# Tokens of a pair of rows split over even and odd partitions, loads reordered, q transposed by the DMA crossbar: a fused linear attention and MLP-mixer kernel on one Trainium2 core

## The chip, the cores and the metric

The kernel runs on one core of a Trainium2 chip. The metric is the device time of one execution in microseconds (us), lower is better. Beside every timed kernel the kernel before is run on the same chip. Its executions fall into two groups, about 321 to 323 us and about 325.5 to 329 us. Runs more than 1.5% above the fastest of the same kernel are called slow here, and only fast runs are compared. The span of a profiled execution is about 1.8 us shorter than its device time.

Engines: PE is TensorE, DVE is VectorE, ACT is ScalarE, POOL is GpSimd, SP is the sync engine, which issues most DMAs. In the traces SP, ACT and POOL each issue to a DMA queue of their own (SPq, ACTq, POOLq). PSUM is the memory that the matmuls write here. The "crossbar" stands for `dma_start_transpose`: a DMA that transposes what it moves. A DMA "lands" when all its data has arrived. The "granted clock" is the share of full speed that TensorE's clock was given.

## The reference

For 8 batches of 576 tokens, with 8 heads of 64 and 1536 channels in the MLP:

```python
r_q, r_k = relu(q), relu(k)                      # [8, 8, 576, 64]
q_p = concat(r_q * cos(pos), r_q * sin(pos))     # 128 features per head
k_p = concat(r_k * cos(pos), r_k * sin(pos))
kv  = sum over tokens of k_p (outer) v ;  z = sum over tokens of k_p
x   = (q_p @ kv) / (q_p . z + 1e-6)              # -> [8, 576, 512], heads side by side
h   = relu(x^T @ w_tok1) @ w_tok2                # mix over tokens
u   = x + h^T
out = u + relu(u @ w_ch1) @ w_ch2                # mix over channels
```

All matmuls are in bf16, inputs and output in float32.

## The kernel before: the parts that matter

576 tokens are 4.5 times 128 partitions. The kernel gives 5 tokens to each of 64 partitions and 4 to each of the other 64. In even batches the 5-token half is partitions 0 to 63, in odd batches 64 to 127, so that two batches' fifth tokens ("tails") together fill 128 partitions for the channel MLP. A tail tile alone has 64 rows.

```python
def halves(c):                        # c = batch % 2
    lo = c * HP                       # HP = 64
    return slice(lo, lo + HP), slice(HP - lo, P - lo)

def load(b, t):                       # two DMAs, two queues, one half each
    A, Bh = halves(b % 2)
    ...
    qB = nc.scalar if b == 0 else nc.gpsimd
    return [nc.sync.dma_start(out=x[A], in_=...),            # 64 partitions x 5 tokens
            qB.dma_start(out=x[Bh, :, :J * D], in_=...)]     # 64 partitions x 4 tokens

def q_turn(self, g):                  # q features -> transposed, for the matmul with kv
    ...
    tr = psA.tile([P, 2 * H, P], BF16, ...)
    for i in range(2 * H):
        nc.tensor.transpose(tr[:, i, :], src[:, i * P:(i + 1) * P], ident)
    nc.scalar.copy(dst, tr)           # 16 PE transposes, one ACT copy out of PSUM
    # g == 2: the tail, 64 rows, 8 transposes

def num(self, j):                     # r is all rows for j < 4, the half A for the tail
    for h in range(H):
        nc.tensor.matmul(nm[r, ...], lw, self.kv[:, h, :D + 1], ...)
```

A period is one batch's channel MLP (48 c_ps matmuls with w_ch1, 48 o_ps matmuls with w_ch2). The attention and the token mixing of the next batch (in the code the steps kv, num, mix1 and mix2, with the tiles kv_ps, nm, b, u_ps and ut_ps) and the q transposes (tr) of the one after are hooked in between, so that PE is always busy. Batch 0 has to be prepared first, and in the first two periods batches 1 and 2 are still being loaded. From batch 2 on, u is transposed by the DMA crossbar; q never is.

## Time and profile before

Device time: 324.75 us median of 4 runs; 321.77 and 322.38 are the fast ones, 327.11 and 327.18 the slow ones. The profiled execution was a fast one. A "third period" below is the third MLP block, counted from its first c_ps matmul. (In the tables of the kernel before and the changed kernel the bounds from the fourth period on come from the chain of waits and lie some 0.16 us later; lengths of whole periods do not change.)

| Stretch of the profiled execution | us | what holds it |
|---|---|---|
| start to the first c_ps | 34.6 | loads of batch 0, then a chain over all engines |
| first period | 46.8 | loads of batch 1, PE clock |
| second period | 40.0 | loads of batches 2 and 3 |
| third period | 32.5 | PE |
| fourth to sixth, each | 30.7 | PE |
| seventh (no q transposes left) | 28.5 | PE |
| the last two blocks and the stores | 46.3 | PE |

The page's head and its slices. A digit is a tenth of busy time in one of 40 slices of the span, PEclk the clock granted to PE in tenths, GB/s what the DMA engines moved:

```profile
span 320.8 us, 5010 instructions
PE 287.4 (90%) x2032; PEld 145.8 (45%) x2056; DVE 165.9 (52%) x326; ACT 141.1 (44%) x184; POOL 62.7 (20%) x97
...
PEclk9789978799999997999999999999999999999999
DMA  7899999910999899914797299622063105302214
GB/s 155 286 140 220 240 259 279 229 25 4 213 281 278 168 264 256 211 42 109 178 255 145 66 231 236 126 65 67 0 67 88 47 0 120 95 0 65 67 36 95
```

PE's 90% is an average over stages with different limits and says little. Two other things are seen: the clock digits 7 and 8 in the first quarter, and the ninth and tenth slice (64 to 80 us), where DMA moves 25 and 4 GB/s although the second period will wait for loads. The stretches from the view by windows (length; busy time and instructions of PE, PEld, DVE, ACT, POOL; granted clock; DMA share; GB/s), for the first, second, fourth and seventh period, confirm it:

```profile
34.57:81.38 46.81, 35.78 (x251) 18.15 (x253) 23.83 (x48) 22.61 (x30) 7.90 (x13) 0.89 0.74 171
81.38:121.40 40.02, 33.51 (x273) 17.61 (x276) 24.57 (x46) 20.96 (x25) 14.94 (x22) 1.00 1.03 242
153.86:184.58 30.72, 30.56 (x235) 15.77 (x236) 17.71 (x36) 17.76 (x23) 6.92 (x10) 1.00 0.73 168
246.03:274.53 28.50, 28.39 (x195) 13.76 (x196) 13.77 (x26) 6.40 (x10) 2.70 (x3) 1.00 0.25 61
```

The chain of waits (start, length, what) has long DMA links before 121 us, and afterwards PE without a break:

```profile
42.17 21.86 DMA w_112<-w_111
...
84.11 20.70 DMA vt<-in_v_dram
...
114.13 7.23 DMA uT<-ub
```

The DMA queue of SP (start, length, what) shows why nothing moved at 64 to 80 us. The load of k for batch 3 stands behind a crossbar transpose that needs the end of the first period:

```profile
78.61 1.28 SPq L314 DMA_TRANSPOSE uT_tail<-utb  x1
80.00 0.65 SPq L76 DMA_DIRECT2D kt<-in_k_dram  x1
```

The rates of the first 20 us, half a microsecond for each number. Batch 0's halves come on two queues, and the rate lies near 210 for five microseconds before it rises:

```profile
GB/s 0 0 0 0 96 78 217 356 229 205 241 233 218 207 203 201 258 332 342 379 390 389 370 376 384 395 386 344 236 13 0 0 0 0 92 179 142 167 58 141
```

### The profile page before, as it was taken

The page shows a single profiled execution, that of the slowest core. Times are in us where ns is not written, and L with a number is a line of the kernel's source. Part 1 is how long each engine was busy: PE and PEld are TensorE (multiplying, and loading weights), DVE is VectorE, ACT ScalarE, POOL GpSimd, SP SyncE. Part 2 cuts the span into 40 slices and gives each one's busy share as a digit, 9 for nine tenths or more (in the row PEclk, how much of TensorE's full clock was granted, in tenths as well). Part 3 has the DMA queues.
Part 4 walks back from the last instruction along what each step waited for, and adds up shares of the span by engine and source line. Part 5 has one row for each costly group of instructions (what it writes and reads, how often), then busy time and mean ns, then how long its engine had stood idle before and what let it go on. Part 6 is the DMA issues. An engine that isn't in the chain of part 4 may idle for free.

```text
span 320.8 us, 5010 instructions
## 1 busy us (share of the span) xinstructions
PE 287.4 (90%) x2032; PEld 145.8 (45%) x2056; DVE 165.9 (52%) x326; ACT 141.1 (44%) x184; POOL 62.7 (20%) x97
## 2 busy tenths in 40 slices
PE   7488874898887978999999999999999999999993
PEld 3263432543553435445544564455455544444441
DVE  0846582237754960666356655765564753332421
ACT  2280439109649142395349445935673420220300
POOL 1077003005510651030602050700020012000000
PEclk9789978799999997999999999999999999999999
DMA  7899999910999899914797299622063105302214
GB/s 155 286 140 220 240 259 279 229 25 4 213 281 278 168 264 256 211 42 109 178 255 145 66 231 236 126 65 67 0 67 88 47 0 120 95 0 65 67 36 95
DMA packets 39127, 45.78 MB, mean 143 GB/s; under 512 B 16448, under 2 KB 33600, under 8 KB 39104
## 3 DMA queue, kind: packets, MB, share of 16 engines
q1 hardware_dynamic: 30880, 29.14, 39.3%
q0 software_dynamic: 6640, 14.75, 21.4%
q10 hardware_dynamic: 1584, 1.57, 1.7%
q8 instruction: 16, 0.26, 0.4%
q14 instruction: 7, 0.06, 0.1%
HBM read 35.78 MB, written 9.44 MB: 141 GB/s over the span
## 4 chain that ended last, share of the span: by engine, by line
PE 70%; DMA 18%; DVE 5%; issue 2%; POOL 2%; ACT 1%; SPq 1%; POOLq 0%; DVEq 0%
PE c_ps L342 25%; PE o_ps L365 23%; DMA w_112<-w_111 7%; DMA vt<-in_v_dram 6%; PE u_ps L295 3%; PE tr L220 3%; PE kv_ps L237 3%; PE nm L253 3%; DMA kt<-in_k_dram 3%; DMA uT<-ub 2%; DVE kp L182 2%; PE o_ps L354 2%; PE ut_ps L308 1%; PE wm L117 1%; POOL vbf_109 L192 1%
## 5 line engine op out<-in xcount | busy, mean ns | idle before, releaser
L342 PE MATMUL c_ps<-uT,wc_117 128*128 128x512 bf16 x384 | 95.9, 387 | 8.4 <-ACT uT L326 2.4
L342 PEld LDWEIGHTS <-wc_117 128*128 128x128 bf16 x432 | 39.4, 99 | 53.6 <-issue 11.9
L207 ACT ACTIVATE qp<-qt,bias_93,cos_t 128x512 bf16<-128x512 f32 (+1 forms) x40 | 31.6, 805 | 17.1 <-DMA qt<-in_q_dram 12.1
L301 POOL CAST ub<-u 128x1024 bf16<-128x1024 f32 x14 | 14.8, 1054 | 122.6 <-DVE u L300 122.6
L368 DVE TENSOR_TENSOR u<-o_ps,u 128x512 f32<-128x512 f32 x28 | 19.3, 691 | 37.5 <-PE o_ps L365 33.6
L221 ACT COPY qpT<-tr 128x2048 bf16<-128x2048 bf16 x16 | 29.9, 1867 | 18.7 <-PE tr L220 18.7
L257 DVE TENSOR_SCALAR den<-nm 128x8 f32<-128x8 f32 (+1 forms) x40 | 6.6, 165 | 42.3 <-PE nm L253 41.8
L261 DVE TENSOR_TENSOR x<-nm,den 128x512 bf16<-128x512 f32 (+1 forms) x40 | 27.6, 691 | 1.4
L182 DVE TENSOR_SCALAR kp<-kt,cos_t 128x512 bf16<-128x512 f32 (+1 forms) x40 | 21.2, 531 | 10.7 <-DMA kt<-in_k_dram 10.7
L207 ACT ACTIVATE qp<-qt,bias_93,sin_t 128x512 bf16<-128x512 f32 (+1 forms) x30 | 24.0, 800 | 0.0
L220 PE MATMUL tr<-ident,qp 128*128 128x128 bf16 x256 | 17.9, 225 | 4.6 <-DVE qp L204 4.4
L182 DVE TENSOR_SCALAR kp<-kt,sin_t 128x512 bf16<-128x512 f32 (+1 forms) x40 | 21.7, 543 | 0.0
L220 PEld LDWEIGHTS <-qp 128*128 128x128 bf16 x256 | 15.9, 101 | 9.2 <-ACT qp L207 5.0
L300 DVE TENSOR_TENSOR u<-u_ps,x 128x1024 f32<-128x1024 f32 x14 | 17.1, 1219 | 2.3 <-PE u_ps L295 2.3
L192 POOL CAST vbf_109<-vt 128x512 bf16<-128x512 f32 (+1 forms) x18 | 11.2, 655 | 31.0 <-DMA vt<-in_v_dram 16.3
L237 PEld LDWEIGHTS <-kp 128*128 128x128 bf16 (+1 forms) x320 | 13.9, 108 | 5.3 <-ACT qpT L221 1.8
L253 PEld LDWEIGHTS <-qpT 128*128 128x128 bf16 x256 | 12.1, 98 | 9.1 <-DVE x L261 2.4
L253 PE MATMUL nm<-kv,qpT 128*128 128x65 bf16 x256 | 13.4, 194 | 1.6 <-DVE x L261 1.6
L117 PE MATMUL wm<-zero 128*128 128x512 bf16 x39 | 12.0, 458 | 2.1 <-DVE zero L111 2.0
L346 ACT ACTIVATE h_2979<-c_ps 128x512 bf16<-128x512 f32 x6 | 3.6, 597 | 21.0 <-PE c_ps L342 21.0
L354 PE MATMUL o_ps<-wc_121,h_429 128*128 128x512 bf16 x45 | 12.5, 396 | 0.2
L365 PE MATMUL o_ps<-wc_121,h_826 128*128 128x512 bf16 x46 | 11.6, 380 | 0.8 <-ACT h_826 L346 0.8
(123 smaller groups left out, 378.0 us busy)
## 6 DMA issues: line engine op xcount, KB each, us to landing
out_dram<-u SPq DMA_DIRECT2D x32, 256.0 KB, 3.3
kt<-in_k_dram SPq DMA_DIRECT2D x8, 640.0 KB, 11.2
qt<-in_q_dram SPq DMA_DIRECT2D x8, 640.0 KB, 14.4
vt<-in_v_dram SPq DMA_DIRECT2D x8, 640.0 KB, 14.5
kt<-in_k_dram POOLq DMA_DIRECT2D x7, 512.0 KB, 6.9
qt<-in_q_dram POOLq DMA_DIRECT2D x7, 512.0 KB, 8.4
vt<-in_v_dram POOLq DMA_DIRECT2D x7, 512.0 KB, 10.5
wc_117<-in_moe_w_ch_dram POOLq DMA_DIRECT2D x3, 512.0 KB, 9.3
```

The costliest lines, as they stand in the source:

```text
L182: nc.vector.tensor_scalar(self.kp[r, j, :, f, :], src, scalar1=tab[r, self.c, j:j + 1], scalar2=0.0, op0=ALU.mult, op1=ALU.max)
L207: nc.scalar.activation(self.qp[r, j, :, f, :], src, AF.Relu, bias=bias0[r], scale=tab[r, self.c, j:j + 1])
L220: nc.tensor.transpose(tr[:, i, :], src[:, i * P:(i + 1) * P], ident)
L221: nc.scalar.copy(dst, tr)
L237: nc.tensor.matmul(kv_ps[:, g, hh * (D + 1):(hh + 1) * (D + 1)], self.kp[r, j, h].rearrange("p f d -> p (f d)"), self.vb[r, j, h, :D + 1], ...
L253: nc.tensor.matmul(nm[r, h // HH, c0:c0 + D + 1], lw, self.kv[:, h, :D + 1], start=True, stop=True)
L261: nc.vector.tensor_mul(self.x[r, j, :].rearrange("p (g h d) -> p g h d", g=2, h=HH), nmv[r, :, :, :D], den_b[r])
L300: nc.vector.tensor_add(self.u[:, js, :], u_ps, self.x[:, js, :])
L342: nc.tensor.matmul(c_ps, wc1[:, ki, mi * P:(mi + 1) * P], uT[:, :, ki, :], start=(ki == 0), stop=(ki == NCC - 1))
L354: nc.tensor.matmul(o_ps[j], h1[:, ki, j * P:(j + 1) * P], wc2[:, ki, :], start=(ki == 0), stop=(ki == NCH - 1))
L365: nc.tensor.matmul(o_ps, h1[:, ki, j * P:(j + 1) * P], wc2[:, ki, :], start=(ki == 0), stop=(ki == NCH - 1))
L368: nc.vector.tensor_add(u[:, j, :], o_ps, u[:, j, :])
```

## The change

Its intent: spread each load over even or odd partitions instead of 64 neighbouring ones; get data into the first two periods sooner; and take the q transposes of batches 3 to 7 off PE and ACT.

Tokens are grouped in 64 runs of 9. A run's 5 and 4 tokens go to a pair of neighbouring partitions. A tail tile now lies on every second partition and is handled as 128 rows, of which 64 are zero.

```diff
-    Q_DMA = ()
+    Q_DMA = range(3, 8)
@@ load
-        return [
-            nc.sync.dma_start(out=x[A], in_=...),
-            qB.dma_start(out=x[Bh, :, :J * D], in_=...),
-        ]
+        for par in (1 - b % 2, b % 2):
+            n, f = count(b % 2, par), first(b % 2)[par]
+            dmas.append(nc.sync.dma_start(
+                out=x[par::2, :, :n * D],
+                in_=src[b].rearrange("h (m r) d -> m h (r d)", r=R)[:, :, f * D:(f + n) * D]))
@@ order of loads
-    after(first w_tok1 load, v0[0])
+    after(first w_tok1 load, q0[1])
 ...  k, q, v of batch 1
+    (copy of w_tok1 for odd batches)        # was behind k, q of batch 2
     w_ch2 in four parts                     # now after q of batch 1
     k, q of batch 2                         # now after part 3 of w_ch2
-    (copy of w_tok1 for odd batches)
@@ q_turn
-            if g < J // 2: ... crossbar or 16 transposes, else: the tail, 64 rows
+        src = self.qp[:, j:j + n] ...
+        if self.b in Q_DMA:
+            nc.sync.dma_start_transpose(out=dst, in_=src)
+            return
@@ kv_mm, num, mix1, mix2: every tail
-            r = self.rows(j)          # 64 rows for the tail
-                nc.tensor.matmul(nm[r, ...], lw, ...)
+                nc.tensor.matmul(nm[:, ...], lw, ...)
@@ start: batch 0
-    s.q_turn(0)                       # 16 transposes at once, later 16 and 8 more
+        s.q_turn(j, 1, psM)           # 8 at a time, between the num steps
@@ first period: v casts, kv and num one or two slots later, and
-        (the load of k, q of batch 3 stood behind the transpose of u_tail)
+        (it stands before it)
```

Cut: the cos and sin tables for the new token places, clearing of the unused tail columns, the same slicing of weights and stores, three v casts of batch 1 that go from POOL to DVE, and the slots of the other hooks.

More of the change, by code (lines that the diff above doesn't have):

```diff
@@ L34 @@
     P = 128
-    HP = P // 2
     J = S // P
     JA = J + 1
-    SA = HP * JA
+    R = J + JA
     NP = B // 2
@@ L44, with first, count @@
     VW = D + 2
-    Q_DMA = ()
+    Q_DMA = range(3, 8)
     U_PE = (0, 1)
-    def halves(c):
-        lo = c * HP
-        return slice(lo, lo + HP), slice(HP - lo, P - lo)
+    def first(c):
+        return (0, JA - c)
+    def count(c, par):
+        return JA if par == c else J
     const = ctx.enter_context(tc.tile_pool(name="const", bufs=1))
@@ L61, with clear, raw_of @@
     ctx.enter_context(tc.manual_schedule())
-    raw = {}
-    def load(b, t):
-        A, Bh = halves(b % 2)
-        if t == "v":
-            x = one.tile([P, H, JA * D], F32, name="vt", tag="vt")
-        else:
-            x = two.tile([P, H, JA * D], F32, name=t + "t", tag=t + "t")
-        src = {"q": q, "k": k, "v": v}[t]
-        raw[t, b] = x
-        qB = nc.scalar if b == 0 else nc.gpsimd
-        return [
-            nc.sync.dma_start(out=x[A], in_=src[b, :, :SA, :].rearrange("h (p j) d -> p h (j d)", j=JA)),
-            qB.dma_start(out=x[Bh, :, :J * D], in_=src[b, :, SA:, :].rearrange("h (p j) d -> p h (j d)", j=J)),
-        ]
+    raw = {(t, i): const.tile([P, H, JA * D], F32, name=f"{t}t{i}") for t, i in
+           (("k", 0), ("q", 0), ("v", 0), ("k", 1), ("q", 1))}
+    def clear(t, i):
+        (nc.gpsimd if t == "q" else nc.vector).memset(raw[t, i][:, :, J * D:], 0.0)
+    for t in "kqv":
+        clear(t, 0)
+    def raw_of(t, b):
+        return raw[t, 0 if t == "v" else b % 2]
+    def load(b, t):
+        x = raw_of(t, b)
+        src = {"q": q, "k": k, "v": v}[t]
+        dmas = []
+        for par in (1 - b % 2, b % 2):
[3 more added lines that the diff above has]
+                in_=src[b].rearrange("h (m r) d -> m h (r d)", r=R)[:, :, f * D:(f + n) * D]))
+        return dmas
     def after(dma, first):
@@ L86 @@
     load(0, "k")
-    load(0, "q")
-    v0 = load(0, "v")
-    pos_i = const.tile([P, 2, JA], mybir.dt.int32, name="pos_i")
-    for c in range(2):
-        A, Bh = halves(c)
-        nc.gpsimd.iota(pos_i[A, c, :], pattern=[[1, JA]], base=0, channel_multiplier=JA)
-        nc.gpsimd.iota(pos_i[Bh, c, :], pattern=[[1, JA]], base=SA, channel_multiplier=J)
+    q0 = load(0, "q")
+    load(0, "v")
+    pos_i = const.tile([P, JA], mybir.dt.int32, name="pos_i")
+    nc.gpsimd.iota(pos_i, pattern=[[2, JA]], base=0, channel_multiplier=R)
+    par_i = const.tile([P, 1], mybir.dt.int32, name="par_i")
+    nc.gpsimd.iota(par_i, pattern=[[0, 1]], base=0, channel_multiplier=1)
+    nc.vector.tensor_single_scalar(par_i, par_i, 1, op=ALU.bitwise_and)
+    par = const.tile([P, 1], F32, name="par")
+    nc.vector.tensor_copy(par, par_i)
+    keep = const.tile([P, 2], F32, name="keep")
+    nc.vector.tensor_scalar(keep[:, 0:1], par, scalar1=-1.0, scalar2=1.0, op0=ALU.mult, op1=ALU.add)
+    nc.vector.tensor_copy(keep[:, 1:2], par)
+    pos = const.tile([P, JA], F32, name="pos")
+    nc.vector.tensor_copy(pos, pos_i)
     theta = const.tile([P, 2, JA], F32, name="theta")
-    nc.vector.tensor_copy(theta, pos_i)
-    scale = (math.pi / 2.0) / S
+    nc.vector.tensor_scalar(theta[:, 0, :], pos, scalar1=par, scalar2=None, op0=ALU.add)
+    nc.vector.tensor_scalar(theta[:, 1, :], pos, scalar1=par, scalar2=None, op0=ALU.subtract)
+    scale = (math.pi / 2.0) / (2 * S)
     sin_t = const.tile([P, 2, JA], F32, name="sin_t")
@@ L106 @@
     nc.scalar.activation(cos_t, theta, AF.Sin, bias=bias_hp, scale=-scale)
+    for tab in (sin_t, cos_t):
+        nc.vector.tensor_mul(tab[:, :, J], tab[:, :, J], keep)
+    clear("k", 1)
+    clear("q", 1)
     ident = const.tile([P, P], BF16, name="ident")
@@ L126 @@
     w1 = [const.tile([P, JA, D_tok], BF16, name=f"w1{c}") for c in range(2)]
-    A, Bh = halves(0)
-    after(nc.gpsimd.dma_start(out=w1[0][A], in_=moe_w_tok1[:SA, :].rearrange("(p j) t -> p j t", j=JA)), v0[0])
-    nc.gpsimd.dma_start(out=w1[0][Bh, :J], in_=moe_w_tok1[SA:, :].rearrange("(p j) t -> p j t", j=J))
+    for c in range(2):
+        nc.gpsimd.memset(w1[c][:, J], 0.0)
+    for par_ in range(2):
+        n, f = count(0, par_), first(0)[par_]
+        d = nc.gpsimd.dma_start(out=w1[0][par_::2, :n],
+                                in_=moe_w_tok1.rearrange("(m r) t -> m r t", r=R)[:, f:f + n, :])
+        if par_ == 0:
+            after(d, q0[1])
     w2r = const.tile([P, NT, S], BF16, name="w2r")
@@ L138 @@
     wc2 = const.tile([P, NCH, Dm], BF16, name="wc2")
-    w2 = const.tile([P, NT, J, 3 * HP], BF16, name="w2")
-    w2a = w2r[:, :, :SA].rearrange("p n (s j) -> p n j s", j=JA)
-    for g in (0, 2):
-        nc.gpsimd.tensor_copy(w2[:, :, :, g * HP:(g + 1) * HP], w2a[:, :, :J, :])
-    nc.gpsimd.tensor_copy(w2[:, :, :, HP:2 * HP], w2r[:, :, SA:].rearrange("p n (s j) -> p n j s", j=J))
-    def load_second():
-        for t in "kqv":
-            d = load(1, t)
-            if t == "k":
-                after(d[0], wc1_dma[1])
+    w2g = w2r.rearrange("p n (m r) -> p n r m", r=R)
+    w2 = const.tile([P, 2, NT, JA, P], BF16, name="w2")
+    nc.gpsimd.memset(w2[:, :, :, J, :], 0.0)
+    for c in range(2):
+        for par_ in range(2):
+            n, f = count(c, par_), first(c)[par_]
+            nc.gpsimd.tensor_copy(w2[:, c, :, :n, par_::2], w2g[:, :, f:f + n, :])
+    def load_second():
+        k1 = load(1, "k")
+        after(k1[0], wc1_dma[1])
+        q1 = load(1, "q")
+        load(1, "v")
+        nc.sync.dma_start(out=w1[1][0::2, :J], in_=w1[0][0::2, :J])
+        nc.sync.dma_start(out=w1[1][1::2, 1:], in_=w1[0][1::2, :J])
+        nc.sync.dma_start(out=w1[1][1::2, 0], in_=w1[0][0::2, J])
+        wc2_dma = []
         for g in range(4):
             n = NCH // 4
-            nc.gpsimd.dma_start(
+            wc2_dma.append(nc.gpsimd.dma_start(
                 out=wc2[:, g * n:(g + 1) * n, :],
-                in_=moe_w_ch2[g * n * P:(g + 1) * n * P, :].rearrange("(n p) c -> p n c", p=P))
-        load(2, "k")
+                in_=moe_w_ch2[g * n * P:(g + 1) * n * P, :].rearrange("(n p) c -> p n c", p=P)))
+        after(wc2_dma[0], q1[0])
+        k2 = load(2, "k")
+        after(k2[0], wc2_dma[2])
         load(2, "q")
-        nc.sync.dma_start(out=w1[1][HP:], in_=w1[0][:HP])
-        nc.sync.dma_start(out=w1[1][:HP, :J], in_=w1[0][HP:, :J])
     u_tail = const.tile([P, NP, Dm], F32, name="u_tail")
@@ L169, in __init__ @@
             self.b, self.c = b, b % 2
-            self.A, self.Bh = halves(self.c)
-        def rows(self, j):
-            return slice(0, P) if j < J else self.A
         def k_feature(self, j, parts=(0, 1)):
@@ L177, in k_feature @@
                 self.kp = one.tile([P, JA, H, 2, D], BF16, name="kp")
-            r = self.rows(j)
-            src = raw["k", self.b][r, :, j * D:(j + 1) * D]
+            src = raw_of("k", self.b)[:, :, j * D:(j + 1) * D]
             for f in parts:
                 tab = (cos_t, sin_t)[f]
-                nc.vector.tensor_scalar(self.kp[r, j, :, f, :], src, scalar1=tab[r, self.c, j:j + 1],
+                nc.vector.tensor_scalar(self.kp[:, j, :, f, :], src, scalar1=tab[:, self.c, j:j + 1],
                                         scalar2=0.0, op0=ALU.mult, op1=ALU.max)
         def v_cast(self, j, eng=nc.gpsimd):
-            r = self.rows(j)
             self.vb = vbf[self.c]
-            src = raw["v", self.b][r, :, j * D:(j + 1) * D]
+            src = raw_of("v", self.b)[:, :, j * D:(j + 1) * D]
             if eng is nc.scalar:
-                eng.copy(self.vb[r, j, :, :D], src)
+                eng.copy(self.vb[:, j, :, :D], src)
             else:
-                eng.tensor_copy(self.vb[r, j, :, :D], src)
+                eng.tensor_copy(self.vb[:, j, :, :D], src)
         def q_feature(self, j, dve=()):
@@ L196, in q_feature @@
                 self.qp = one.tile([P, JA, H, 2, D], BF16, name="qp")
-                self.qpT = two.tile([P, J * H, P], BF16, name="qpT")
-                self.qpTt = two.tile([P, H, HP], BF16, name="qpTt")
-            r = self.rows(j)
-            src = raw["q", self.b][r, :, j * D:(j + 1) * D]
+                self.qpT = two.tile([P, JA * H, P], BF16, name="qpT")
+            src = raw_of("q", self.b)[:, :, j * D:(j + 1) * D]
             for f in range(2):
@@ L203, in q_feature, with q_turn @@
                 if f in dve:
-                    nc.vector.tensor_scalar(self.qp[r, j, :, f, :], src, scalar1=tab[r, self.c, j:j + 1],
+                    nc.vector.tensor_scalar(self.qp[:, j, :, f, :], src, scalar1=tab[:, self.c, j:j + 1],
                                             scalar2=0.0, op0=ALU.mult, op1=ALU.max)
                 else:
-                    nc.scalar.activation(self.qp[r, j, :, f, :], src, AF.Relu, bias=bias0[r],
-                                         scale=tab[r, self.c, j:j + 1])
-        def q_turn(self, g):
-            if g < J // 2:
-                src = self.qp[:, 2 * g:2 * g + 2].rearrange("p j h f d -> p (j h f d)")
-                dst = self.qpT[:, 2 * g * H:(2 * g + 2) * H, :]
-                if self.b in Q_DMA:
-                    nc.sync.dma_start_transpose(out=dst, in_=src)
-                    return
-                tr = psA.tile([P, 2 * H, P], BF16, name="tr", tag="psA")
-                for i in range(2 * H):
-                    nc.tensor.transpose(tr[:, i, :], src[:, i * P:(i + 1) * P], ident)
-                nc.scalar.copy(dst, tr)
-            else:
-                src = self.qp[self.A, J].rearrange("p h f d -> p (h f d)")
-                tr = psA.tile([P, H, HP], BF16, name="trt", tag="psA")
-                for i in range(H):
-                    nc.tensor.transpose(tr[:, i, :], src[:, i * P:(i + 1) * P], ident[self.A, self.A])
-                nc.scalar.copy(self.qpTt, tr)
+                    nc.scalar.activation(self.qp[:, j, :, f, :], src, AF.Relu, bias=bias0,
+                                         scale=tab[:, self.c, j:j + 1])
+        def q_turn(self, j, n, psum=psA):
+            src = self.qp[:, j:j + n].rearrange("p j h f d -> p (j h f d)")
+            dst = self.qpT[:, j * H:(j + n) * H, :]
+            if self.b in Q_DMA:
+                nc.sync.dma_start_transpose(out=dst, in_=src)
+                return
+            tr = psum.tile([P, n * H, P], BF16, name="tr", tag="psA" if psum is psA else "psM")
+            for i in range(n * H):
+                nc.tensor.transpose(tr[:, i, :], src[:, i * P:(i + 1) * P], ident)
+            nc.scalar.copy(dst, tr)
         def kv_mm(self):
@@ L232, in kv_mm @@
             for j in range(JA):
-                r = self.rows(j)
                 for g in range(2):
@@ L237, in kv_mm @@
                         nc.tensor.matmul(kv_ps[:, g, hh * (D + 1):(hh + 1) * (D + 1)],
-                                         self.kp[r, j, h].rearrange("p f d -> p (f d)"),
-                                         self.vb[r, j, h, :D + 1],
+                                         self.kp[:, j, h].rearrange("p f d -> p (f d)"),
+                                         self.vb[:, j, h, :D + 1],
                                          start=(j == 0 and hh == 0), stop=(j == J and hh == HH - 1),
@@ L247, in num @@
                 self.x = two.tile([P, JA, Dm], BF16, name="x")
-            r = self.rows(j)
             nm = psA.tile([P, 2, 512], F32, name="nm", tag="psA")
             for h in range(H):
-                lw = self.qpT[:, j * H + h, :] if j < J else self.qpTt[:, h, :]
+                lw = self.qpT[:, j * H + h, :]
                 c0 = (h % HH) * (D + 1)
-                nc.tensor.matmul(nm[r, h // HH, c0:c0 + D + 1], lw, self.kv[:, h, :D + 1],
+                nc.tensor.matmul(nm[:, h // HH, c0:c0 + D + 1], lw, self.kv[:, h, :D + 1],
                                  start=True, stop=True)
@@ L256, in num @@
             den = small.tile([P, 2, HH, 1], F32, name="den")
-            nc.vector.tensor_scalar_add(den[r], nmv[r, :, :, D:], 1e-6)
-            nc.vector.reciprocal(den[r], den[r])
+            nc.vector.tensor_scalar_add(den, nmv[:, :, :, D:], 1e-6)
+            nc.vector.reciprocal(den, den)
             den_b = bass.AP(tensor=den.tensor, offset=den.offset,
                             ap=[den.ap[0], [HH, 2], [1, HH], [0, D]])
-            nc.vector.tensor_mul(self.x[r, j, :].rearrange("p (g h d) -> p g h d", g=2, h=HH),
-                                 nmv[r, :, :, :D], den_b[r])
+            nc.vector.tensor_mul(self.x[:, j, :].rearrange("p (g h d) -> p g h d", g=2, h=HH),
+                                 nmv[:, :, :, :D], den_b)
         def mix1(self, j, psum=None):
@@ L271, in mix1 @@
                     self.b1 = [psum.tile([P, Dm], F32, name="b1", tag="psM") for mi in range(NT)]
-            r = self.rows(j)
             for mi in range(NT):
-                nc.tensor.matmul(self.b1[mi], w1[self.c][r, j, mi * P:(mi + 1) * P], self.x[r, j, :],
+                nc.tensor.matmul(self.b1[mi], w1[self.c][:, j, mi * P:(mi + 1) * P], self.x[:, j, :],
                                  start=(j == 0), stop=(j == J))
@@ L294, in mix2 @@
                     for ki in range(NT):
-                        nc.tensor.matmul(u_ps[:, jj], w2[:, ki, 2 * g + jj, self.c * HP:self.c * HP + P],
+                        nc.tensor.matmul(u_ps[:, jj], w2[:, self.c, ki, 2 * g + jj, :],
                                          self.B1[:, ki, :], start=(ki == 0), stop=(ki == NT - 1))
@@ L304, in mix2 @@
             else:
-                i, A = self.b // 2, self.A
+                i = self.b // 2
                 ut_ps = psA.tile([P, Dm], F32, name="ut_ps", tag="psA")
                 for ki in range(NT):
-                    nc.tensor.matmul(ut_ps[A], w2r[:, ki, J:SA:JA], self.B1[:, ki, :],
+                    nc.tensor.matmul(ut_ps, w2[:, self.c, ki, J, :], self.B1[:, ki, :],
                                      start=(ki == 0), stop=(ki == NT - 1))
-                nc.vector.tensor_add(u_tail[A, i, :], ut_ps[A], self.x[A, J, :])
+                if self.c == 0:
+                    nc.vector.tensor_add(u_tail[:, i, :], ut_ps, self.x[:, J, :])
+                else:
+                    nc.vector.tensor_add(u_tail[:, i, :], ut_ps, u_tail[:, i, :])
+                    nc.vector.tensor_add(u_tail[:, i, :], u_tail[:, i, :], self.x[:, J, :])
                 if self.c == 1:
@@ L370, in channel, with out_rows @@
                 step()
-    def out_rows(b, js):
-        A, Bh = halves(b % 2)
-        return ((A, out[b, :SA, :].rearrange("(p j) c -> p j c", j=JA)[:, js, :]),
-                (Bh, out[b, SA:, :].rearrange("(p j) c -> p j c", j=J)[:, js, :]))
+    def out_rows(b, par, j, n):
+        f = first(b % 2)[par] + j
+        return out[b].rearrange("(m r) c -> m r c", r=R)[:, f:f + n, :]
     def store_batch(b):
@@ L379, in store @@
             if j % 2:
-                for r, dst in out_rows(b, slice(j - 1, j + 1)):
-                    nc.sync.dma_start(out=dst, in_=u[r, j - 1:j + 1, :])
+                for par in range(2):
+                    nc.sync.dma_start(out=out_rows(b, par, j - 1, 2), in_=u[par::2, j - 1:j + 1, :])
         return store
@@ L385, in store_tail @@
         for c in range(2):
-            A, _ = halves(c)
-            nc.sync.dma_start(out=out[2 * j + c, J:SA:JA, :], in_=u[A, j, :])
+            nc.sync.dma_start(out=out_rows(2 * j + c, c, J, 1), in_=u[c::2, j:j + 1, :])
     bt = [Batch(b) for b in range(B)]
@@ L404 @@
     s.kv_mm()
-    s.q_turn(1)
     s.num(0)
+    s.q_turn(2, 1, psM)
     s.num(1)
-    s.q_turn(2)
+    s.q_turn(3, 1, psM)
+    s.num(2)
+    s.q_turn(4, 1, psM)
+    s.mix1(0, psM)
+    s.num(3)
+    s.mix1(1)
     keep_warm(2)
-    s.mix1(0, psM)
-    s.num(2)
-    s.mix1(1)
-    s.num(3)
+    s.num(4)
     s.mix1(2)
     keep_warm(2)
-    s.num(4)
     s.mix1(3)
@@ L420 @@
     s.mix1_out(split=True)
-    keep_warm(4)
+    keep_warm(3)
     load_second()
@@ L436, in first_hooks @@
             at(1 + j, n.k_feature, j)
-            at(6 + j // 2, n.q_feature, j, dve=(1,))
-            at(9, n.v_cast, j, nc.gpsimd if j < 3 else nc.scalar)
-        at(9, n.q_turn, 0)
-        at(10, n.q_turn, 1)
-        at(11, n.q_turn, 2)
-        at(11, n.kv_mm)
+            at(5 + j, n.q_feature, j, dve=(1,))
+        at(7, n.q_turn, 0, 2)
+        at(9, n.q_turn, 2, 2)
+        at(11, n.q_turn, 4, 1)
+        for j in range(JA):
+            at(11, n.v_cast, j, nc.vector if j < 3 else nc.scalar)
         at(12, load, 2, "v")
+        at(13, n.kv_mm)
         for j in range(JA):
-            at(13 + j, n.num, j)
-            at(15 + j, n.mix1, j)
-        at(19, n.mix1_out, split=True)
-        at(20, n.mix2, 0)
-        at(21, n.mix2, 1)
-        at(22, n.mix2, 2)
+            at(14 + j, n.num, j)
+            at(16 + j, n.mix1, j)
+        at(20, n.mix1_out, split=True)
+        at(21, n.mix2, 0)
+        at(22, n.mix2, 1)
+        at(23, n.mix2, 2)
         for j in range(JA):
@@ L464, in second_hooks @@
             at(j, n.v_cast, j)
-        for g in range(3):
-            at(2 + g, n.q_turn, g)
+        at(2, n.q_turn, 0, 2)
+        at(3, n.q_turn, 2, 2)
+        at(4, n.q_turn, 4, 1)
         at(5, n.kv_mm)
@@ L480, in second_hooks @@
             at(14 + g, n.mix2, g)
-            at(16 + g, m.q_turn, g)
+        at(16, m.q_turn, 0, 2)
+        at(17, m.q_turn, 2, 2)
+        at(18, m.q_turn, 4, 1)
         return h
@@ L508, in hooks_for @@
                 at(13 + j, m.k_feature, j)
-            at(12, m.q_turn, 0)
-            at(15, m.q_turn, 1)
-            at(16, m.q_turn, 2)
+            at(12, m.q_turn, 0, 2)
+            at(15, m.q_turn, 2, 2)
+            at(16, m.q_turn, 4, 1)
         return h
```

## The prediction

> **What bounds the kernel now.** From 121 us on, TensorE: in the chain of waits every piece from there to 316 us is PE. Four 128x512 matmuls take 0.86 us; a period (one batch's channel MLP with the next batch's attention) takes 30.7 us (184.6, 215.3, 246.0), and the one without q transposes, 246.03 to 274.53, 28.5. Before 121 us, loads: the first c_ps starts at 34.6 us; the first period lasts 46.8 us, the second 40.0, against about 31 of PE work each. The chain goes through DMA w1 copy (21.9 us), DMA vt (20.7) and DMA uT (7.2); the timeline has PE gaps of 2.4, 2.9, 1.7, 1.3 and 2.4 us in the first period, and the granted clock is 0.72 at 52 to 64 us.
>
> The loads are slow for two reasons, by the DMA view over short windows. (1) A load writes partitions 0-63 from one queue and 64-127 from another. The rate sits at 200 to 240 GB/s for long stretches and only sometimes at 340 to 410. [...]I read 205 GB/s as one half in flight alone and 400 as both; the trace agrees with a factor of two, though not at 3 to 8 us, where both halves run at 215. (2) SP stands in order behind the transpose of u_tail: k3 is issued only at 80.0 us, and DMA is nearly idle at 66 to 80 us.
>
> **What the change does.** [...]I expect 300 to 380 GB/s for loads. Loads go whole, in one queue; k3 and q3 stand before the u_tail transpose; weights start after q0, not v0 (15.7 us).
> It removes 40 PE transposes from each of five batches (2.2 us of PE, 4.3 us of ACT copies) and adds 1.3 MB of crossbar transposes per batch. The u transposes show 256 KB at 290 GB/s and 1.25 us of SP time each: about 4.5 us of DMA and 6 of SP per batch (estimate), in periods whose DMA need is then about 24 of 28.5 us. Tail tiles become 128 rows: PE time unchanged (194 against 197 ns).
>
> **Critical path.**
> - Start: k lands 1 to 3 us earlier, a 16-block transpose leaves the way before num; first c_ps at about 30 us (-4.5).
> - First period: about 36 us (-11); what stays is ACT's ten q features before its u copies at the end, a PE gap of 2 to 3 us.
> - Second period: about 32 us (-8), 2.2 of it batch 3's transposes.
> - Four more periods at 28.5 us (-9); the last three blocks unchanged.
>
> Span about 320.8 - 32 = 288 us, device time about 290.
>
> **Prediction.** 290 us, 281 to 303 in 8 of 10. Faster by over 2%: 0.95; within 2%: 0.04; slower: 0.01.
>
> **What would show it.** Granted clock 0.95 or more in the first period; DMA over 300 GB/s while loads run; no long PE wait on w1 or vt; third period starting near 98 us; later periods 28.5 us with no PE gap before num; q transposes landing in 3 to 6 us.
>
> **What would make it wrong.** q transposes landing late, behind loads or stores in SP's order, so that num waits (up to 5 us a period); one queue alone not exceeding 205 to 240 GB/s, so that the start gains nothing and batch 1 is still late (+8); ACT or DVE, not PE, pacing the dense first two periods (+5); or DMA saving more in the start than I count (-6).

What the trace of the kernel before shows are rates of 200 to 240 GB/s and at times 340 to 410. The reading "205 as one half, 400 as both" was a guess about these rates, and the 300 to 380 GB/s expected of the change were the author's estimate. The sum: -4.5 - 11 - 8 - 9 = -32.5, rounded to -32. "Ports" in the texts stands for the choice of partitions; no run shows ports as such.

## The result, and the profile after

The changed kernel takes 290.06 us (median of 4 runs, 289.65 to 290.8, all fast; correct output). The ratio to the kernel before is 0.901, with a 95% interval of 0.898 to 0.904. A ratio here is the mean time of one kernel's fast runs over that of the other's fast runs of the same rounds, so it is not quite the ratio of the medians quoted.

The page's head and slices after:

```profile
span 289.0 us, 4658 instructions
PE 264.6 (92%) x1836; PEld 133.1 (46%) x1855; DVE 173.8 (60%) x344; ACT 120.3 (42%) x171; POOL 53.8 (19%) x77
...
PEclk9999999999899999999999999999999999999999
DMA  6999999992795399999969994970494043003012
GB/s 210 286 160 210 349 257 221 357 312 96 246 303 179 81 204 231 364 159 255 314 212 204 241 360 114 211 169 0 76 232 95 2 91 126 20 2 145 0 63 83
```

The clock is full almost everywhere. The first, second, third and fourth period in the view by windows:

```profile
32.27:70.28 38.01, 32.02 (x249) 16.80 (x252) 24.96 (x51) 22.59 (x30) 7.92 (x11) 1.00 0.91 257
70.28:104.33 34.05, 31.94 (x234) 16.24 (x236) 23.86 (x47) 16.85 (x22) 9.49 (x14) 0.95 0.69 207
104.33:132.51 28.18, 27.82 (x195) 13.89 (x197) 18.75 (x36) 13.44 (x20) 6.22 (x8) 1.00 1.04 248
132.51:160.09 27.58, 27.48 (x195) 13.89 (x196) 18.24 (x36) 13.44 (x20) 5.26 (x7) 1.00 0.90 241
```

The DMA rates of the first 20 us stay near 360 as long as q, k and v of batch 0 are loaded, and those loads end at 13 us instead of 14.5:

```profile
GB/s 0 0 0 0 53 43 186 360 387 385 399 393 323 331 369 363 363 369 363 363 352 346 359 364 353 218 36 0 102 147 180 168 68 85 141 185 163 182 195 182
```

The chain of waits has only two DMA links of any length left, at the change from the second to the third period. Of the 5.86 us of the second, PE sits idle for 0.26 us only:

```profile
100.84 3.45 DMA uT<-ub
...
104.94 5.86 DMA qpT<-qp
```

The stretches side by side give the balance in us: the start 34.57 to 32.27 (-2.3), the first period 46.81 to 38.01 (-8.8), the second 40.02 to 34.05 (-6.0), the third to seventh together from 153.1 to 138.5 (-14.6), the rest unchanged. The sum is the -31.8 of the spans.

### The profile page after: what moved, and what is told of

Its sections match the earlier page's. It is cut to its first block, busy times and chain, and to the rows that moved or that the text cites. A ratio compares the mean times of both kernels' runs of the same rounds, so it can differ in the third digit from the quotient of the medians.

```text
span 289.0 us, 4658 instructions
## 1 busy us (share of the span) xinstructions
PE 264.6 (92%) x1836; PEld 133.1 (46%) x1855; DVE 173.8 (60%) x344; ACT 120.3 (42%) x171; POOL 53.8 (19%) x77
## 4 chain that ended last, share of the span: by engine, by line
PE 66%; DMA 3%; ACT 2%; DVE 2%; issue 1%; POOL 0%; POOLq 0%; DVEq 0%
PE c_ps L362 27%; PE o_ps L385 26%; PE u_ps L311 3%; PE nm L270 2%; PE kv_ps L255 2%; DMA qpT<-qp 2%; ACT qpT L246 1%; DMA uT<-ub 1%; PE ut_ps L324 1%; PE b_2640 L290 1%; PE b_1705 L290 1%; PE b_1386 L290 1%; PE b_2335 L290 1%; PE b_2020 L290 1%; PE b_1052 L290 1%
## 5 line engine op out<-in xcount | busy, mean ns | idle before, releaser
L278 DVE TENSOR_TENSOR x<-nm,den 128x512 bf16<-128x512 f32 x40 | 27.7, 691 | 1.4
L274 DVE TENSOR_SCALAR den<-nm 128x8 f32<-128x8 f32 x40 | 6.6, 165 | 27.0 <-PE nm L270 27.0
L233 ACT ACTIVATE qp<-qt_76,bias_106,cos_t 128x512 bf16<-128x512 f32 x20 | 15.9, 804 | 6.5 <-DMA qt_76<-in_q_dram 6.5
L316 DVE TENSOR_TENSOR u<-u_ps,x 128x1024 f32<-128x1024 f32 x14 | 17.1, 1220 | 2.5 <-PE u_ps L311 2.5
L246 ACT COPY qpT<-tr 128x1024 bf16<-128x1024 bf16 (+1 forms) x11 | 14.4, 1327 | 7.2 <-PE tr L245 7.1
L233 ACT ACTIVATE qp<-qt_79,bias_106,cos_t 128x512 bf16<-128x512 f32 x20 | 15.9, 804 | 0.0
L245 PE MATMUL tr<-ident,qp 128*128 128x128 bf16 x120 | 8.8, 219 | 4.3 <-ACT qp L233 2.8
L211 DVE TENSOR_SCALAR kp<-kt_75,cos_t 128x512 bf16<-128x512 f32 x20 | 11.3, 563 | 2.0 <-DMA kt_75<-in_k_dram 2.0
L255 PEld LDWEIGHTS <-kp 128*128 128x128 bf16 x320 | 11.2, 97 | 2.5 <-DVE kp L211 0.8
L366 ACT ACTIVATE h_2764<-c_ps 128x512 bf16<-128x512 f32 x6 | 3.6, 597 | 20.6 <-PE c_ps L362 20.6
L233 ACT ACTIVATE qp<-qt_79,bias_106,sin_t 128x512 bf16<-128x512 f32 x15 | 12.0, 803 | 0.0
L233 ACT ACTIVATE qp<-qt_76,bias_106,sin_t 128x512 bf16<-128x512 f32 x15 | 12.0, 802 | 0.0
L374 PE MATMUL o_ps<-wc_140,h_448 128*128 128x512 bf16 x45 | 11.8, 378 | 0.2
L220 POOL CAST vbf_126<-vt_77 128x512 bf16<-128x512 f32 x15 | 10.1, 714 | 9.3 <-PE kv_ps L255 9.2
```

The lines of the kernel that those rows point to most:

```text
L233: nc.scalar.activation(self.qp[:, j, :, f, :], src, AF.Relu, bias=bias0, scale=tab[:, self.c, j:j + 1])
L255: nc.tensor.matmul(kv_ps[:, g, hh * (D + 1):(hh + 1) * (D + 1)], self.kp[:, j, h].rearrange("p f d -> p (f d)"), self.vb[:, j, h, :D + 1], ...
L278: nc.vector.tensor_mul(self.x[:, j, :].rearrange("p (g h d) -> p g h d", g=2, h=HH), nmv[:, :, :, :D], den_b)
L316: nc.vector.tensor_add(self.u[:, js, :], u_ps, self.x[:, js, :])
L374: nc.tensor.matmul(o_ps[j], h1[:, ki, j * P:(j + 1) * P], wc2[:, ki, :], start=(ki == 0), stop=(ki == NCH - 1))
```

## The experiments

Every kernel gave a correct output. "Span" is that of the profiled execution, which was a fast one except where said. A period starts with the first c_ps matmul of its block. For order_only, old_order and before_crossbar the kept trace, used in the last two columns, is of another execution than the one noted with the result (spans 313.3, 306.8 and 334.3 us). The medians contain slow runs for halves_two_queues and parity_two_queues (fast ones alone: mean 345.8 and 317.8 us) and for before_crossbar (325.7).

| Run | layout | queues of a load | tail rows | order | q of 3 to 7 | us (median) | ratio to before | span | start of third period |
|---|---|---|---|---|---|---|---|---|---|
| before | halves | 2 | 64 | old | PE | 321 to 327 | 1 | 320.8 | 121.4 |
| order_only | halves | 2 | 64 | new | PE | 315.9 | 0.982 | 315.5 | 118.0 |
| old_order | even/odd | 1 | 128 | old | PE | 308.0 | 0.955 | 305.6 | 112.5 |
| pe_transpose | even/odd | 1 | 128 | new | PE | 299.1 | 0.925 | 298.3 | 105.2 |
| after | even/odd | 1 | 128 | new | crossbar | 290.1 | 0.901 | 289.0 | 104.3 |
| halves | halves | 1 | 128 | new | crossbar | 312.8 | 0.968 | 311.5 | 112.9 |
| halves_tail64 | halves | 1 | 64 | new | crossbar | 313.1 | 0.969 | 314.2 | 113.5 |
| halves_two_queues | halves | 2 | 128 | new | crossbar | 349.5 | 1.080 | 341.5 | 116.1 |
| parity_two_queues | even/odd | 2 | 128 | new | crossbar | 320.4 | 0.986 | 314.8 | 106.5 |
| two_queues_after_turns | even/odd | 2, waits | 128 | new | crossbar | 291.3 | 0.902 | 289.9 | 105.4 |
| before_crossbar | halves | 2 | 64 | old | crossbar | 326.2 | 1.013 | 333.2, a slow run | 120.2 |

### What are the partitions worth? (halves)

```diff
+    def side(par): return slice(par * 64, par * 64 + 64)
-                out=x[par::2, :, :n * D],
+                out=x[side(par), :, :n * D],
     (and the same for weights, stores and the cos and sin tables)
```

> The changed kernel, but the two tokens groups of a pair lie on partitions 0-63 and 64-127 instead of even and odd ones; order, single queue, 128-row tails and crossbar transposes as changed. Theory (ports): loads run near 205 GB/s instead of 360, v of batch 0 lands near 20 us instead of 13, first c_ps near 37 us instead of 32.3, batch 1 is late, and the first two periods lose 5 to 10 us more; the later periods stay at 27.6 us, or a little over. Span 299 to 308 us. Rival (the new order of loads alone repaired the front): span within 3 us of 289.

Measured: 312.8 us, ratio 0.968; 22.7 us more than the changed kernel. The sizes of all transfers and their order are the same. The rates of the first 20 us:

```profile
GB/s 0 0 0 0 61 109 240 350 222 213 246 223 215 207 204 199 246 223 217 215 221 248 223 210 205 207 202 252 215 220 214 221 256 210 210 212 213 220 185 204
```

The partitions set the rate here, as the theory has it: 200 to 250 GB/s where even and odd partitions gave 320 to 400. The effect was larger than expected (299 to 308), because the later periods did not stay at 27.6. The fourth, fifth and sixth take 31.7, 30.0 and 33.7 us, and those with the most waiting show it as a wait for crossbar transposes. Around such waits for transposes PE's granted clock fell too (0.95 and 0.90 in the fourth and sixth). That loads at 215 instead of 360 GB/s leave too little DMA time for the transposes is read from the views (DMA share 1.10 in the fourth period against 0.90 in the changed kernel) and not tested by itself. So the layout does not only help the front; the crossbar's part of the change seems to need it too. On halves the runs with the crossbar (312.8 and 313.1) are only about 3 us faster than order_only with its transposes on PE (315.9), though the number of queues differs as well; on even and odd partitions the crossbar gives 9.

### Or was it the number of queues? (halves_two_queues, then parity_two_queues)

```diff
-            dmas.append(nc.sync.dma_start(
+            eng = nc.sync if par == 1 - b % 2 else (nc.scalar if b == 0 else nc.gpsimd)
+            dmas.append(eng.dma_start(
```

> As halves, but the second half of each load is issued from another queue (ACT for batch 0, POOL after), as in the kernel before. Theory (ports): both halves in flight at times, so rates change between 205 and 400 GB/s, and the time lies between: span 292 to 301 us. Rival (it is the number of queues, not the partitions, that sets the rate): as fast as the changed kernel, 289.

Measured: 349.5 us (fast runs 343.3 and 348.4), slower than the kernel before by 8%. Both sides were wrong about the time. The second queue brought no steady 400 GB/s, and the chain of waits has links of 18.1, 24.6 and 14.7 us of q transposes, in which PE sat idle for up to 9.2, 15.0 and 3.5 us at a stretch. The same edit on the changed kernel tells layout from queue:

> The changed kernel with one edit: the second group of each load comes from another queue (ACT for batch 0, POOL after), as halves_two_queues did, but on even and odd partitions. Theory A (loads from the POOL queue beside crossbar transposes on SP hold the transposes back, whatever the partitions): q transposes land after 10 us or more, TensorE waits for them, 300 us or more. Theory B (it was the half layout that left no room): q transposes land in 4 to 6 us, 289 to 295 us.

Measured: 320.4 us (fast runs 316.6 and 319.1; these are 28 us above one queue). Theory A held. The loads of the first 20 us still run near 360 GB/s, so the layout does its work with two queues as well. What breaks is the transposes. SP's queue at the end of the second period, and POOL's:

```profile
104.49 13.94 SPq L242 DMA_TRANSPOSE qpT<-qp  x3
```

```profile
105.69 0.69 POOL L85 DMA_DIRECT2D kt<-in_k_dram  x1 [2.56 <-DVE kp L212]
106.37 0.69 POOL L85 DMA_DIRECT2D qt<-in_q_dram  x1
```

The chain of waits there, in which PE sits idle for 13.88 us:

```profile
104.49 22.85 DMA qpT<-qp x2
```

In the changed kernel SP issues the next loads behind the transposes in the same queue (transposes from 102.19, loads from 110.98 us). POOL's program does not wait for them and issues its part as soon as the buffers are free (at 105.69 us here), into the middle of the transposes (104.49 to 127.34 us). The three transposes of that batch land after 6.6, 20.7 and 13.3 us. Those of batches 6 and 7, beside which POOL has no loads left, need 3.1 to 6.5.

### Is it the overlap, or the queue itself? (two_queues_after_turns)

```diff
+            if turns and par == b % 2:
+                after(dmas[1], turns[-1])      # POOL's load waits for the last q transpose
```

> parity_two_queues with one more dependency: from batch 6 on, the part of a load that POOL issues waits until the q transposes of the period before have landed. Theory (the transposes are slow because POOL's loads are in flight at the same time[...]): q transposes after the first batch land in 4 to 6 us, the third and later periods return to 28 to 29 us, 296 to 306 us in all (the transposes of batch 3 still overlap). Rival (a second queue slows the transposes or the loads in itself, overlapping or not): 314 us or more.

Measured: 291.3 us (290.6 to 292.1), ratio 0.902. The landing times of the q transposes (shortest, median, longest; first the two queues, then the two queues with the wait, then the changed kernel):

```profile
DMA to landing us min/median/max: 3.1/4.8/20.7
```

```profile
DMA to landing us min/median/max: 3.1/4.4/6.4
```

```profile
DMA to landing us min/median/max: 3.1/4.5/6.4
```

So a second queue costs 1 us in itself, and the overlap costs about 27 (fast runs: 317.8 against 291.3). The expectation named the wrong batch: the dependency holds from batch 5 on, so it already covers the loads beside batch 3's transposes (4.4, 6.4 and 4.7 us to landing), which is why the result is below the expected 296 to 306. The cause of the slowness inside the DMA engines is not shown by these runs.

### The crossbar alone, and the transposes put back on PE (before_crossbar, pe_transpose)

```diff
-    Q_DMA = ()                 # kernel before
+    Q_DMA = range(3, 8)
```

> The kernel before, with one edit: q of batches 3 to 7 (tokens 0 to 3; the tail stays on TensorE) transposed by the crossbar. Theory (the crossbar needs the room on the DMA queues that the even/odd layout makes; with loads in halves on two queues it waits behind them): the later periods lose 1.9 us of PE work but wait for q, so no gain or a loss: 318 to 345 us. Rival (the transposes are worth their PE time wherever they are moved): 5 times 1.9 us less, 312 to 313 us for a run of 322.

Measured: 326.2 us, ratio 1.013 (1.009 to 1.017): a small loss. Both profiled runs were slow ones and are not compared. But in them, too, q transposes land after up to 20.6 and 17.2 us. What the transposes saved on PE was lost again, it seems in these waits.

```diff
-    Q_DMA = range(3, 8)        # changed kernel
+    Q_DMA = ()
```

> The changed kernel with all q transposes on TensorE again. Theory (transposes cost 2.2 us of PE in each of 5 periods, and the rest of the later periods' gain, 0.9 us each, comes from the 128-row tails): the periods that had 27.6 us take 29.8, span 299 to 301 us. Rival (all 3.1 us of a period's gain are transposes): 30.7 us a period, span 304.

Measured: 299.05 us, 9 us more than the changed kernel. The fourth period:

```profile
135.00:164.82 29.82, 29.66 (x235) 16.13 (x236) 17.85 (x36) 18.09 (x23) 4.87 (x7) 1.00 0.55 173
```

29.82 us is 2.24 above the changed kernel's 27.58, the PE time of 40 transposes, and 0.90 below the 30.72 of the kernel before, which has the same transposes. So the later periods gained from two things, not one.

### The tail tiles (halves_tail64)

```diff
+            r = slice(0, P) if j < J else side(self.c)
-                nc.tensor.matmul(nm[:, ...], self.qpT[:, ...], ...)
+                nc.tensor.matmul(nm[r, ...], self.qpT[:, ..., r], ...)
     (and the same for kv, mix1 and mix2 at the fifth token)
```

> As halves, with the matmuls of the tail tiles (kv, num, mix1, mix2 at the fifth token) on 64 rows or columns as in the kernel before; the instruction counts stay. Theory (changing the array's tile size costs TensorE some 0.1 us at each of about 8 changes in a period): periods of 28.5 us instead of 27.6, and 5 to 7 us more than halves in all. Rival (tile size costs nothing, as 194 against 197 ns of one matmul suggest): the same as halves within 1 us.

(The theory's 0.1 us at each of about 8 changes is an estimate: together they make up the 0.9 us a period that the transposes' 2.2 leave of the gain of 3.1.)

Measured: 313.1 us against 312.8, no difference in the whole, as the rival had it. But that whole is ruled by DMA waits, which can absorb it. The seventh period has no loads and no transposes, so it is ruled by PE alone. Here it is first in halves, then in halves_tail64:

```profile
237.34:264.93 27.59, 27.48 (x195) 13.90 (x196) 14.30 (x27) 6.39 (x10) 2.69 (x3) 1.00 0.47 89
```

```profile
239.18:267.63 28.45, 28.34 (x195) 13.65 (x196) 13.77 (x26) 6.39 (x10) 2.69 (x3) 1.00 0.46 87
```

The instruction counts of PE are the same (195 matmuls, 196 weight loads), and the difference is 0.86 us. Where it arises is seen in PE's timeline of that period (start, length, what). First halves_tail64, then halves:

```profile
240.04 1.54 PE L267 MATMUL kv_ps<-vbf,kp 128*128 128x65 bf16 x40
241.51 1.90 PE L372 MATMUL c_ps<-uT,wc 128*128 128x512 bf16 x8
...
247.82 0.44 PE L283 MATMUL nm<-kv,qpT 128*64 128x65 bf16 x8
248.20 1.04 PE L372 MATMUL c_ps<-uT,wc 128*128 128x512 bf16 x4
```

```profile
238.21 1.43 PE L262 MATMUL kv_ps<-vbf,kp 128*128 128x65 bf16 x40
239.48 1.89 PE L369 MATMUL c_ps<-uT,wc 128*128 128x512 bf16 x8
...
245.68 0.42 PE L277 MATMUL nm<-kv,qpT 128*128 128x65 bf16 x8
245.94 1.02 PE L369 MATMUL c_ps<-uT,wc 128*128 128x512 bf16 x4
```

From kv's start to the next c_ps it is 1.47 us with the 64-row tail and 1.27 without. From the tail's nm to the next c_ps it is 0.38 and 0.26, and 0.09 more are lost before that nm. The tails of mix1 (1.06 against 0.86 us to the next c_ps) and of mix2 (0.21 us before and after ut_ps) lose as much. Each of the four places thus costs 0.20 to 0.21 us, 0.82 of the 0.86. The single matmul is about as long as before (eight of the tail's nm take 0.44 and 0.42 us); the time goes where the tile size changes, 0.86 us a period. Why a change costs time is not shown. Half of the rows of a tail are now zeros, and it is still faster by these 0.86 us.

### The order of loads, on either layout (order_only, old_order)

order_only is halves_tail64 with the loads on two queues and Q_DMA empty, so only the order differs from the kernel before in what matters here. old_order is pe_transpose with the old order of loads, start and first period put back. "Order" here means all three together.

> The new order of loads and of the first two periods alone: halves on two queues, 64-row tails, q on TensorE, as in the kernel before. Theory (order and ports each repair a part of the front; periods stay at 30.7): front shorter by 3 to 9 us, span 312 to 318. Rival (the order does nothing without the ports): within 2 us of 321.

> The changed layout (even and odd partitions, 128-row tails, one queue) with the old order of loads, of the first two periods and of the start, and q on TensorE. Against pe_transpose (299) it tells what the new order is worth[...]. Theory: third period starts 5 to 10 us later than the 105 us of pe_transpose, span 303 to 309. Rival (with loads at 360 GB/s the order no longer matters): 298 to 301.

Measured: order_only 315.9 us, ratio 0.982 (0.980 to 0.984); old_order 308.0 us (304.9 to 309.1), ratio 0.955. Both came out inside what the theories expected. By the medians of fast runs the order is worth 5.8 us on the old layout (321.6 to 315.85) and 9.0 on the new one (308.0 to 299.05, from different rounds; old_order's own runs spread over 4 us). Faster loads do not make the order unnecessary: with the old order the first period still lasts 46.0 us at a granted clock of 0.89 in one profile and 43.2 us at 0.96 in another, against 37.8 us in pe_transpose.

### What is left in the front (fix_start, fix_both, fix_q2)

The front gained less than predicted, so its waits were looked up. ACT in the changed kernel, at the start (start, length, what, and in brackets the idle time before and what ended it):

```profile
13.62 1.01 ACT L246 COPY qpT<-tr 128x1024 bf16<-128x1024 bf16 x1 [2.10 <-PE tr L245]
14.52 0.81 ACT L233 ACTIVATE qp<-qt_76,bias_106,cos_t 128x512 bf16<-128x512 f32 x1
16.05 1.01 ACT L246 COPY qpT<-tr 128x1024 bf16<-128x1024 bf16 x1 [0.71 <-PE tr L245]
16.96 2.22 ACT L233 ACTIVATE qp<-qt_76,bias_106,cos_t 128x512 bf16<-128x512 f32 x3
19.08 0.58 ACT L260 CAST kv<-kv_ps 128x520 bf16<-128x520 f32 x1
```

The first transpose waits for the warm-up matmuls on PE (26 matmuls of zeros, 7.9 us; no run tells what they are worth), which start only at 5.2 us (2.0 before) because DVE writes their zeros after its new table work and clearing. ACT's program then alternates between features and copies, so the wait is passed on until the cast of kv, which all of num needs. And at the end of the first period ACT computes ten q features (7 us) before the u copies that PE waits for:

```profile
70.28 4.44 PE L362 MATMUL c_ps<-uT,wc_136 128*128 128x512 bf16 x12 [2.54 <-ACT uT L346]
```

After this gap 12 matmuls take 4.44 us: the granted clock of that stretch is 0.62. The length of the gap alone does not decide that. In the kernel before, the clock of the 4.5 us after a gap of 2.29 us (119.1 to 121.4) is 0.62 too, but after one of 2.41 us (79.0 to 81.4) it is 1.00. What decided is not shown.

```diff
-    for j in range(2):
-        s.q_feature(j, dve=(1,)); s.q_turn(j, 1, psM)
-    keep_warm(4)
-    for j in range(2, JA): s.q_feature(j, dve=(1,))
+    for j in range(JA): s.q_feature(j, dve=(1,))      # fix_start
+    for j in range(2): s.q_turn(j, 1, psM)
+    keep_warm(4)
@@ fix_both as well: q features of batch 2
-        for j in range(JA): at(21, n2.q_feature, j)   # end of the first period
+        for j in range(3): at(21, n2.q_feature, j)    # 3 and 4 at the start of the second
```

> Only the first of the two repairs of fix_both (all q features of batch 0 before its transposes). Its share: first c_ps at 30.3 us instead of 32.3, about 2 us of the 3.3 us that fix_both gained, so 288 us; if the start were absorbed by a later load, 290.

> The changed kernel with two repairs of the front: all q features of batch 0 are emitted before its transposes, so that ACT does not wait for the warm-up matmuls and casts kv sooner (about 0.9 us); and q features 3 and 4 of batch 2 move from the end of the first period, where ACT does ten of them (7 us) before the u copies that TensorE waits 2.5 us for, to the start of the second (about 1.5 us, and up to 1.5 more if the TensorE clock no longer drops after that gap). Theory: 285 to 288 us. Rival (something else paces the front): 289.5 to 290.5.

> fix_both with q of batch 2 on the crossbar too. Theory: the second period loses another 2.2 us of PE work, 284.5 us. Rival (that period is paced by the chain behind num, its features or the ub casts, not by PE): 286 to 287.

Measured: fix_start 288.3 us, first c_ps at 30.0 us; fix_both 286.8 us (286.4 to 287.7), first c_ps at 30.25 and the gap at the end of the first period 1.10 us; fix_q2 287.9 us. fix_both is faster than both kernels, ratio 0.893 (0.891 to 0.895); the changed kernel had 0.901 (0.898 to 0.904). Its granted clock is 1.00 in the first two periods. fix_q2 gained nothing, so its rival was right about the time. Its second period lasts 34.8 us against 33.6 in fix_both. First fix_both, then fix_q2:

```profile
66.71:100.33 33.62, 30.68 (x236) 15.81 (x236) 25.20 (x49) 19.41 (x26) 10.90 (x17) 1.00 0.70 214
```

```profile
66.59:101.36 34.77, 28.41 (x194) 13.59 (x196) 25.51 (x49) 15.09 (x23) 10.89 (x16) 1.00 0.91 245
```

PE has 2.27 us less to do and waits for it instead. In fix_q2 ACT starts the next batch's q features only at 80.36 us, when the last crossbar transpose of batch 2 has landed (80.29; both use the one qp tile). The relus of h stand behind these features, and PE waits for them for 0.91 and 2.30 us, which it does not in fix_both. So the transposes' PE time was saved, and a new wait took it. The run does not show that PE's work did not matter before.

## Why the prediction was right

The total was 290.06 us for 290.0 predicted. The mechanism held: faster and earlier loads in front, transposes off PE behind. The closeness of the number is luck: two terms that were off in opposite directions, by 6.4 and 5.6 us, cancelled.

- **Start.** Predicted first c_ps "at about 30 us (-4.5)", measured 32.27 (-2.3). That k came earlier was right: DVE's first k feature starts at 7.18 instead of 8.94 us. Mis-sized was what follows: ACT standing behind the warm-up matmuls was not seen. fix_start moves the first c_ps to 30.0 by emission order alone.
- **First period.** Predicted 36 us, measured 38.0. The gap of 2 to 3 us behind ACT's ten q features was predicted and is there (2.54). Missing from the sum were further PE gaps of 0.88, 0.58 and 0.98 us between 39 and 46 us, ended by q features of DVE and ACT; the case "ACT or DVE, not PE, pacing" had been named only among what could go wrong. A granted clock over 0.95 was right (1.00).
- **Second period.** Predicted 32, measured 34.05, with the clock at 0.95 after the gap and 1.28 us of waiting for u's transpose at its end. The third period therefore starts at 104.3 us, not "near 98".
- **Later periods.** Predicted "28.5 us", measured 27.58. The transposes' term was right: 2.2 predicted, 2.24 by pe_transpose. The step that failed is "Tail tiles become 128 rows: PE time unchanged (194 against 197 ns)". It compared the lengths of single matmuls, and these are indeed equal. What changed is the time between them, 0.86 us a period by halves_tail64 and 0.90 by pe_transpose against before. The third to seventh period gained 14.6 us together, where the prediction had 9 for four of them. The sum closes: 9.0 for transposes (4 x 2.24), 4.5 for five tails, and 1.7 by which the third period before was longer than the fourth (its granted clock was 0.95), less 0.6 of waits in the third period after.
- **Balance.** The start and the first two periods gained 17.1 instead of 23.5 us, the later ones 14.6 instead of 9.
- **Load rates.** The rate of 300 to 380 GB/s was right: near 360 while loads run alone. That one queue suffices was left open in the prediction, and is so (near 360 with one queue as with two). The reading "400 as both", that the rate depends only on whether both halves are in flight, does not hold up. Two queues on halves gave 215 at 3 to 8 us and about 340 at 9 to 14 us in the same start (halves_two_queues), and why it is so is open.
- **Crossbar.** "q transposes landing in 3 to 6 us" was right (3.1 to 6.4). The reason that it is so was not in the prediction: the loads stand behind the transposes in the same queue. parity_two_queues and two_queues_after_turns showed that this order matters. "Lost behind loads or stores in SP's order" was feared from the wrong side: with the loads in SP's order the transposes landed after 6.4 us at most, with half of them outside it after up to 20.7.

## What to carry to other kernels

Look at where a transfer's partitions lie before tuning its order: the same bytes ran at about 215 or 360 GB/s here. Ask also what else the DMA engines carry when work is moved to them, and in which queue: the same crossbar transposes gained 9 us with the loads behind them in one ordered queue, and with half of the loads issued freely from a second queue the kernel was 28 us slower than that. Tiles of 64 rows between tiles of 128 cost 0.86 us a period here, which no single matmul shows; compare whole stretches with equal instruction counts, not instruction lengths.
